# Planning the main slots and turning their first tokens inside the early slots, with early weights loaded at every second step

## The chip, the core and the metric

The kernel runs on one core of a Trainium2 chip. TensorE (PE) multiplies matrices; a weight load (PEld) goes ahead of each matmul. VectorE (DVE), ScalarE (ACT) and GpSimd (POOL) work on tiles, SyncE (SP) issues plain transfers, and POOL issues the indirect ones. Each engine works through its own queue in order. The metric is device time in microseconds (us) for one execution, lower is better.

## The reference

Linear attention over 8 batches, 8 heads, 576 tokens and 64 dimensions, followed by a mixture of 8 experts in which each token goes to one expert.

```python
def phi(x):                       # 64 -> 256 features
    proj = x @ w_phi
    proj = proj - max(abs(proj))
    return concat([exp(proj), exp(-proj)])
kv = phi(k).T @ v;  z = sum(phi(k))
attn = phi(q) @ kv / (phi(q) @ z + 1e-6)

x = attn as (8, 576, 512)
logits = x @ w_gate;  local = sigmoid(x @ w_local)
# token s of a batch: the argmax expert if s == 0 or local < 0.5,
# else the expert of the token before
p = softmax(logits)
out[b, s] = p[e] * (relu(x[b, s] @ w1[e]) @ w2[e])     # 512 -> 1024 -> 512
```

All numbers are float32. The kernel works the expert products as sums of three products of rounded parts (hi x hi, hi x lo, lo x hi).

## The kernel before

**Attention, 72 steps.** The tokens are handled in chunks of 128; 9 chunks make a pair of batches, and 4 pairs of batches by 4 pairs of heads give 144 chunks, two per `step`. A step projects (`proj`), turns, exponentiates (`qtr`, `qexp`), sums keys into values (`kv`), and takes matmuls of the numerator from a list (`num`); the result `xo` goes to HBM (`xs`), and POOL adds its gate columns to the logits `lg` (L421 to L424). In this stage PE's order is the program's.

**Gates.** When a pair of batches is done, `gate` runs as a generator in the background, one piece at a step (`chores`): the expert of each token, its rank among the tokens of that expert, its probability. POOL then scatters token numbers and probabilities into a list in HBM that is sorted by expert (`lst`, nine indirect transfers, L657). The fourth gate runs after the last step: `ends` keeps it as `last_gate`, and `advance` (called `go` in `run`) and `rest` push it on from inside the expert work.

**Early slots.** After the second gate half of the tokens have their experts. `plan_early` fills two slots (e0, e1) of three units of 128 tokens of one expert, to be worked while the rest is not yet known. It reads the list by an indirect gather into `lr` (`fetch`, L722), and turns the list with two PE transposes (L735) `WAIT` steps later. `early_chores` advances the early weights (`early_weights`) at each step: SP loads a piece of 512 KB into `wraw`, and one step later ScalarE copies the high part (`whi`, L935) and POOL subtracts for the low part (`wlo`, L937, four operations). The six gathers of tokens (`xg`, L964) follow, one per step. POOL's transfers in the background begin behind a small copy of the current step's maximum (`paced`, L518), so that they keep in step.

**Expert slots.** `slots` works through a list of slots: `layer1` (512 to 1024, relu into `hh` and its rest `hl`), `layer2` (1024 to 512, one PSUM tile `l2` for each unit, then `y` on VectorE and an indirect write to `out`, L1103). In pauses between matmuls these call functions from a list: the next slot's tokens are turned there (`tokens`, L990, into `xhi`, `xlo`), and what `run` passes in `soon` (pauses of the first layer) and `later` (behind the tokens, in the second layer). `used` and `spare` load and split the next slot's weights, one piece for each piece that is done with; 11 pairs of buffers in the early slots, 13 in the main ones. Into what memory a piece comes first also depends: with `ml1` open, every other `wraw` is there, in memory that the list tile had.

**Main slots.** `plan_main` starts from the final counts and works out, in about a hundred small VectorE operations (L745 to L866), which expert each of the main slots has and where its tokens stand, gathers the list again and turns it. Before, its first part was called at the last pause of e0's second layer and its second part at the fifth pause of e1's first layer. Then `moe` began: it gathered the first main slot's tokens, loaded its weights, turned its tokens, and went on with slots of 4, 3, 2 and 1 units.

Outside the 72 steps a planner orders each engine's queue ahead of time from the program's order and its own estimate of when inputs are ready, so a call's place in the program is the earliest, not always the final place of its instructions.

Of the kernel before, what the change touches and what calls it, by code (L numbers as in the profile page):

```python
# [7 lines left out]
F32 = mybir.dt.float32  # L8
# [19 lines left out]

GATE_T = -1.5 * 2.0 ** -23

WAIT, HOLD = 2, 2
PLACE = 16
LAG = 1
WE, WR, WL = 8, 3, 2
# [21 lines left out]
class Kernel:  # L56
# [9 lines left out]
    def run(self):  # L66
        nc, tc, A = self.nc, self.tc, self.A
        act, dve = self.act, self.dve
        with ExitStack() as root:
# [66 lines left out]
            front.close()  # L136
            self.open_main(root)
            plan = self.plan_main()

            def more():  # L140
                with tc.high_priority():
                    next(plan, None)
            go = self.advance

            def rest():
                for _ in self.last_gate:
                    pass
            no = lambda: None
            self.slots(self.eslots, soon=[[no, no, no, go, no, no, go, no, no, go, rest], [no, no, no, no, more]],
                       later=[[no, no, more]])  # L150
            back.close()
            self.open_rest(root)
            self.moe()
# [228 lines left out]
    def num(self, u, b, cs, kvs, bank=None):  # L382
# [23 lines left out]
        def end():  # L406
            last()
            dve, pool, t = self.dve, self.pool, e["t"]
            for c in cs:
                del self.ch[u * NC + c]  # L410
            rc = self.back2.tile([128, 3, 2], F32, name="rc", bufs=3)[:, 0:n]
            dve.tensor_scalar_add(rc, t[:, :, DEN], 1e-6)
            dve.reciprocal(rc, rc)
            xo = self.back2.tile([128, 3, 2 * KV], F32, name="xo", bufs=4)[:, 0:n]
            dve.tensor_mul(xo.rearrange("p c (h k) -> p c h k", h=2), t.rearrange("p c (h k) -> p c h k", h=2),
                           rc.unsqueeze(3).broadcast_to([128, n, 2, KV]))
            if hp == 0 and c0 == 0:
                self.lg[bp] = self.back2.tile([128, NC, 9], F32, name="lg")
            lg, ga, gb = self.lg[bp][:, c0:c0 + n], xo[:, :, 0:9], xo[:, :, 2 * KV - 9:2 * KV]
            if hp == 0:  # L420
                pool.tensor_add(lg, ga, gb)  # L421
            else:
                pool.tensor_add(lg, lg, ga)
                pool.tensor_add(lg, lg, gb)  # L424
# [18 lines left out]

    def early_chores(self, s, f):

        w = self.early_weights()
        for x in f:
            next(w, None)
            yield x
        for x in s:  # L450
            for u in range(x["n"]):
                with self.paced():
                    self.gather_x(x, u)
                next(w, None)
                yield STEP
        for _ in w:
            yield STEP
# [54 lines left out]
    def paced(self):  # L512


        if self.tail:
            return nullcontext()
        t = self.small.tile([128, 1], F32, name="tick", bufs=2)
        return self.tc.issue_after(self.pool.tensor_copy(t, self.m[:, 0:1]).ins)  # L518

# [16 lines left out]
    def gate(self, bp):  # L536
# [9 lines left out]
            return ap.unsqueeze(1).broadcast_to([128, NC, E])  # L546

        lt = self.lg.pop(bp)
        L = lt[:, :, 0:E]
        mx = sm([128, NC], "mx")  # L550
        dve.tensor_reduce(mx, L, AX.X, ALU.max)
# [148 lines left out]
    def fetch(self, es, k, n, name, wait, halves=()):  # L700
# [11 lines left out]
            yield STEP  # L712
        full = n
        if halves:
            n, halves = n + DUALS, halves()
        lr = self.small.tile([NU + DUALS, 128 * PLACE], F32, name="lr")[0:n]
        parts = [(lr[0:full], 128, ri[0:full, :])]
        w = 64 * PLACE
        parts += [(lr[full:n, w * z:w * z + w], 64, r[0:DUALS, :]) for z, r in enumerate(halves)]
        for o, b, r in parts:  # L720
            with self.paced():
                ins = pool.indirect_dma_start(o, None, self.lst.rearrange("(u n) t -> u (n t)", n=b),  # L722
                                              bass.IndirectOffsetOnAxis(r, 0))
            for x in self.scattered:
                self.tc.add_manual_dep(ins.ins, x.name, mybir.DependencyInfo(
                    mybir.DependencyClass.Sync, mybir.DependencyReason.DATA), reason="the list is read")
        self.scattered = []
        for _ in range(wait):
            yield STEP
# [61 lines left out]
    def plan_main(self):  # L791
# [75 lines left out]
            return rh  # L867

        f = self.fetch(es, k, NU, "m", 1, duals)
        next(f)  # L870
        yield
        try:
# [4 lines left out]
        self.by_size = {}  # L877
        for n, cap in SIZES:
            self.by_size[n], at = [], FIRST[n]
            for i in range(cap):  # L880
                self.by_size[n].append(dict(ei=[ei[at:at + 1]], tok=tok, prob=prob, u=at, n=n, name=f"m{at}", rows=NT + 1))
                at += n
        self.ds = [dict(ei=[x[i:i + 1] for x in eh], tok=tok, prob=prob, u=NU + i, n=1, name=f"d{i}", rows=NT + 1)
                   for i in range(DUALS)]


    def open_main(self, root):
# [193 lines left out]
    def layer2(self, s, between, held=None):  # L1081
        tc, dve, pool = self.tc, self.dve, self.pool
        hh, hl = s["h"]
        for k in range(s["n"]):
            self.l2n = getattr(self, "l2n", 0) + 1
            p = self.psr if hasattr(self, "psr") and self.l2n % 3 else self.psm4
            t = p.tile([128, DM], F32, name="l2")
            o = slice(k * 128, k * 128 + 128)
            for f in range(8):
                c = slice((f % 2) * DM, (f % 2) * DM + DM)  # L1090
# [20 lines left out]

    def slots(self, order, held=None, soon=(), later=()):
        first = order[0]
        for f in self.tokens(first):
            f()
        self.held = len(first.get("w", ()))
        self.coming = list(order)
        for i, s in enumerate(order):
# [149 lines left out]
```

## Time and profile before

| | us |
|---|---|
| runs, each alone | 771.33, 777.69, 777.87 |
| median of these | 777.69 |
| profiled execution, whole | 769.31 |
| its span, first to last instruction | 767.5 |
| TensorE busy in the span | 738.5 |
| VectorE, ScalarE, POOL busy | 449.8, 342.6, 181.8 |
| mean granted TensorE clock | 0.991 |

The profile is one execution. A row of a timeline gives the start, the duration, the engine, the line of the kernel, the operation with output and inputs, and in brackets the time that the engine stood idle ahead of it with what ended the idle time. In the windows each engine's busy time in a stretch is followed by the granted clock (1.00 is full speed) and by the share of time for which the 16 DMA engines were busy. Matmuls overlap, so the duration of one is more than its share of time.

### The profile page before, as it was taken

What the parts mean: (1) busy time and instruction counts of PE and PEld (TensorE: products, weight loads), DVE (VectorE), ACT (ScalarE), POOL (GpSimd) and SP (SyncE); (2) the same over time, 40 slices, a digit from 0 to 9 for tenths busy, and PEclk for the clock granted to TensorE, in tenths of its full rate; (3) what the DMA queues carried; (4) which work ended last, traced back from release to release, by engine and by line L of the source; (5) the groups of instructions that cost most, each with busy time, mean ns of one, the idle gap of its engine ahead of it and who ended that gap; (6) DMA issues with size and microseconds to landing.
All of it is one profiled execution on the core that took longest, in us unless ns stands there. A gap on an engine that the chain in (4) does not pass through costs nothing. (4 is left out here: it accounts for less than half of the span.)

```text
span 767.5 us, 21973 instructions
## 1 busy us (share of the span) xinstructions
PE 738.5 (96%) x9319; PEld 636.8 (83%) x9319; DVE 449.8 (59%) x828; ACT 342.6 (45%) x648; POOL 181.8 (24%) x307
## 2 busy tenths in 40 slices
PE   7999999999897999998999999999999999999996
PEld 6999989989897988887768985788888778878895
DVE  5888888789886887564652247435323554544411
ACT  4776667656785574313541136314212453433300
POOL 0210103301595441525302130021202102101011
PEclk9999999999998999999999999999999999999999
DMA  7755545544777614115923977432397464432000
GB/s 201 239 169 141 152 122 147 154 126 138 238 227 233 188 38 127 65 43 196 364 90 110 358 293 267 150 124 82 124 352 282 142 243 165 138 123 97 1 38 29
DMA packets 66100, 125.04 MB, mean 163 GB/s; under 512 B 7220, under 2 KB 45300, under 8 KB 65950
## 3 DMA queue, kind: packets, MB, share of 16 engines
q1 hardware_dynamic: 57808, 101.03, 40.5%
q0 software_dynamic: 8016, 22.51, 8.3%
q8 instruction: 74, 1.21, 0.6%
q14 instruction: 26, 0.21, 0.1%
q10 hardware_dynamic: 176, 0.07, 0.0%
HBM read 102.05 MB, written 22.06 MB: 162 GB/s over the span
## 5 line engine op out<-in xcount | busy, mean ns | idle before, releaser
L935 ACT CAST whi<-wraw 128x1024 fp32r<-128x1024 f32 x88 | 92.1, 1048 | 127.2 <-PE l L1005 51.9
L937 DVE TENSOR_TENSOR wlo<-wraw,whi 128x1024 fp32r<-128x1024 f32 x80 | 97.7, 1224 | 86.7 <-ACT whi L935 86.7
L1004 PE MATMUL l<-xhi,whi 128*128 128x384 f32 (+2 forms) x352 | 126.0, 358 | 2.2 <-DVE hl L1044 1.8
L1006 PE MATMUL l<-xhi,wlo 128*128 128x384 f32 (+2 forms) x352 | 123.9, 352 | 0.0
L1005 PE MATMUL l<-xlo,whi 128*128 128x384 f32 (+2 forms) x352 | 123.6, 351 | 0.0
L1004 PE MATMUL l<-whi,hh 128*128 128x512 f32 x288 | 117.4, 407 | 2.4 <-DVE y L1100 1.6
L1006 PE MATMUL l<-whi,hl 128*128 128x512 f32 x288 | 114.4, 397 | 0.0
L1005 PE MATMUL l<-wlo,hh 128*128 128x512 f32 x288 | 114.2, 396 | 0.0
L276 ACT ACTIVATE kp<-sb 128x512 f32<-128x512 f32 x144 | 83.7, 629 | 57.9 <-DVE sb L272 55.1
L270 DVE TENSOR_REDUCE m<-pj 128x8 f32<-128x1024 f32 x72 | 87.8, 1219 | 36.0 <-PE pj L267 34.4
L1043 ACT ACTIVATE hh<-l 128x384 fp32r<-128x384 f32 (+1 forms) x84 | 44.9, 534 | 132.4 <-PE l L1006 132.4
L300 ACT ACTIVATE qp<-pj 128x512 f32<-128x512 f32 x144 | 80.3, 596 | 33.6 <-PE pj L285 10.4
L267 PE MATMUL pj<-first,kq 64*128 64x128 f32 x1152 | 86.9, 292 | 6.9 <-DMA kq<-in_kqT 4.1
L272 DVE TENSOR_TENSOR sb<-pj,m 128x1024 f32<-128x1024 f32 x72 | 88.1, 1224 | 3.4
L395 PE MATMUL nm<-kvs,qp 128*64 128x74 f32 x2304 | 87.5, 229 | 1.4 <-ACT kvs L375 1.4
L1044 DVE SCALAR_TENSOR_TENSOR hl<-l,hh 128x384 fp32r<-128x384 f32 (+1 forms) x84 | 51.4, 612 | 59.4 <-ACT hh L1043 59.4
L267 PEld LDWEIGHTS pj<-first,kq 64*128 64x128 f32 x1152 | 73.0, 194 | 13.9 <-ACT ks L364 4.3
L395 PEld LDWEIGHTS nm<-kvs,qp 128*64 128x64 f32 x2304 | 80.1, 138 | 2.4 <-ACT kvs L375 2.1
L317 PE MATMUL kvp<-v,kp 128*64 128x65 f32 x2048 | 78.8, 228 | 1.4 <-issue 0.9
L1004 PEld LDWEIGHTS l<-xhi,whi 128*128 128x128 f32 x352 | 66.1, 188 | 16.7 <-issue 5.2
L1103 POOL DMA_INDIRECT out<-y,p_tokm x30 | 34.4, 1147 | 179.7 <-DVE y L1100 164.7
L317 PEld LDWEIGHTS kvp<-v,kp 128*64 128x64 f32 x2048 | 68.4, 140 | 5.3 <-ACT kp L276 1.4
(222 smaller groups left out, 922.5 us busy)
## 6 DMA issues: line engine op xcount, KB each, us to landing
wraw<-in_w1h SPq DMA_DIRECT2D x44, 512.0 KB, 6.6
wraw<-in_w2h SPq DMA_DIRECT2D x44, 512.0 KB, 3.7
kq<-in_kqT SPq DMA_DIRECT2D x47, 384.0 KB, 4.0
v<-in_va SPq DMA_DIRECT2D x48, 195.0 KB, 3.7
xs<-xo SPq DMA_DIRECT2D x48, 128.0 KB, 3.4
whi<-in_w1h SPq DMA_DIRECT2D x8, 512.0 KB, 7.0
wlo<-in_w1h SPq DMA_DIRECT2D x8, 512.0 KB
whi<-in_w2h SPq DMA_DIRECT2D x8, 512.0 KB, 4.0
```

The source lines that it names most:

```text
L267: self.last_pe = self.pe.matmul(t[:, h, i % 2, j, :], kq[r, j, s], self.w2[r], start=True, stop=True)
L270: dve.tensor_reduce(m, f, AX.X, ALU.max, apply_absolute_value=True)
L272: self.last_dve = dve.tensor_sub(sb.rearrange("p h c j f -> p (h c j) f"), f, m.unsqueeze(2).broadcast_to([128, 8, 128]))
L276: self.last_act = act.activation(kp[:, :, :, sg, :].rearrange("p c h f -> p h c f"), sb[:, :, :, 0], AF.Exp, scale=1.0 - 2 * sg)
L300: self.act.activation(qp[:, sg].rearrange("p h (c r k) -> p (h c) r k", c=2, r=2), src, AF.Exp, scale=1.0 - 2 * sg)
L317: self.pe.matmul(t[r, sg, h], kp[:, h, sg, r], v[:, h], start=first and sg + h == 0, stop=last and sg + h == 2)
L395: self.pe.matmul(e["t"][r, c - c0, k], self.ch[i]["qp"][:, sg, h, q0 + r.start:q0 + r.stop], kvs[:, sg, k], start=sg == 0, stop=sg == 1)
L935: self.act.copy(hi, raw)
L937: (low or self.dve).tensor_sub(lo[:, c], raw[:, c], hi.bitcast(F32)[:, c])
L1004: mm(o, ah, bh, start=first, stop=False)
L1005: mm(o, ah, bl, start=False, stop=False)
L1006: self.last_pe = mm(o, al, bh, start=False, stop=last)
```

## The change

The plan's first two parts are called at the first pause of e0's second layer (`listed`), which also puts the first main slot on the list of slots whose weights come next; its third part (`read`) at the third pause of e1's first layer; the first main slot's tokens are gathered at the fifth (`ahead`) and turned in e1's second layer from the third pause on. Functions in `later` now come ahead of the next slot's tokens. `slots` turns its first slot's tokens only if that has not been done. The slots' descriptions are made before the list is fetched, and the gathers for the half units are issued behind the full one. The second layer's tile of the early slots comes from the pool `psb` (two banks) and no longer from `psm4` (one bank). The early weights advance at every second step, `WAIT` is 3, a gate's first part waits one more step during attention, and after the last step `paced` puts transfers behind the last logit addition.

```diff
-WAIT, HOLD = 2, 2
+WAIT, HOLD = 3, 2
...
-            def more():
-                with tc.high_priority():
-                    next(plan, None)
...
+            def listed():
+                next(plan)
+                next(plan)
+                self.coming.append(self.by_size[4][0])
+
+            def read():
+                with tc.high_priority():
+                    next(plan, None)
             no = lambda: None
-            self.slots(self.eslots, soon=[[no, no, no, go, no, no, go, no, no, go, rest], [no, no, no, no, more]],
-                       later=[[no, no, more]])
+            m = []
+
+            def ahead():
+                m.append(self.tokens(self.by_size[4][0], True))
+            self.slots(self.eslots, soon=[[no, no, no, go, no, no, go, no, no, go, rest], [no, no, read, no, ahead]],
+                       later=[[listed], [no, no] + [lambda k=k: m[0][k]() for k in range(4)]])
...
-                pool.tensor_add(lg, lg, gb)
+                self.last_pool = pool.tensor_add(lg, lg, gb)
...
-        w = self.early_weights()
+        w, k = self.early_weights(), 0
         for x in f:
-            next(w, None)
+            if k % 2 == 0:
+                next(w, None)
+            k += 1
             yield x
...
-                next(w, None)
+                if k % 2 == 0:
+                    next(w, None)
+                k += 1
                 yield STEP
...
         if self.tail:
-            return nullcontext()
+            return self.tc.issue_after(self.last_pool.ins)
...
         lt = self.lg.pop(bp)
+        if not self.tail:
+            yield STEP
...
+        gather(lr[0:full], 128, ri[0:full, :])
+        if halves:
+            for z, r in enumerate(halves()):
+                gather(lr[full:n, w * z:w * z + w], 64, r[0:DUALS, :])
...
         f = self.fetch(es, k, NU, "m", 1, duals)
+        self.by_size = {}
...
+        yield
         next(f)
         yield
...
-            p = self.psr if hasattr(self, "psr") and self.l2n % 3 else self.psm4
-            t = p.tile([128, DM], F32, name="l2")
+            if hasattr(self, "psr"):
+                t = (self.psr if self.l2n % 3 else self.psm4).tile([128, DM], F32, name="l2")
+            else:
+                t = self.psb.tile([128, DM], F32, name="l2", tag="nm")
...
-        for f in self.tokens(first):
-            f()
+        if "x" not in first:
+            for f in self.tokens(first):
+                f()
...
             if i < len(later):
-                rest = rest + list(later[i])
+                rest = list(later[i]) + rest
```

More of the change, by code (lines that the diff above doesn't have):

```diff
@@ L714, in fetch, with gather @@
         if halves:
-            n, halves = n + DUALS, halves()
+            n = n + DUALS
         lr = self.small.tile([NU + DUALS, 128 * PLACE], F32, name="lr")[0:n]
-        parts = [(lr[0:full], 128, ri[0:full, :])]
         w = 64 * PLACE
-        parts += [(lr[full:n, w * z:w * z + w], 64, r[0:DUALS, :]) for z, r in enumerate(halves)]
-        for o, b, r in parts:
+        def gather(o, b, r):
             with self.paced():
@@ L869, in plan_main @@
         f = self.fetch(es, k, NU, "m", 1, duals)
+        self.by_size = {}
+        for n, cap in SIZES:
+            self.by_size[n], at = [], FIRST[n]
+            for i in range(cap):
+                self.by_size[n].append(dict(ei=[ei[at:at + 1]], u=at, n=n, name=f"m{at}", rows=NT + 1))
+                at += n
+        yield
         next(f)
@@ L876, in plan_main @@
         self.tok, self.prob, self.eim, self.eih = tok, prob, ei, eh
[L877 to L884, printed above, removed]
+        self.ds = [dict(ei=[x[i:i + 1] for x in eh], u=NU + i, n=1, name=f"d{i}", rows=NT + 1) for i in range(DUALS)]
+        for x in [x for n, _ in SIZES for x in self.by_size[n]] + self.ds:
+            x.update(tok=tok, prob=prob)
     def open_main(self, root):
```

## The prediction

> **What bounds the kernel now.** I read the page's totals first, then PE's busy time in long and in short windows, then what ended PE's waits, and last the queues that feed those waits.
>
> ```profile
> span 767.5 us, 21973 instructions
> PE 738.5 (96%) x9319; PEld 636.8 (83%) x9319; DVE 449.8 (59%) x828; ACT 342.6 (45%) x648; POOL 181.8 (24%) x307
> ```
>
> TensorE is the bound: it is busy for 738.5 of 767.5 us, so all that an edit of order can win lies in 29 us of gaps, and in time that PE spent at a lower clock. The windows (PE, PEld, DVE, ACT, POOL busy, then granted clock and DMA share) say where these are.
>
> ```profile
> 205.00:235.00 30.00, 28.24 (x721) 26.65 (x721) 21.15 (x34) 24.64 (x51) 28.46 (x53) 1.00 0.77 235
> 235.00:240.00 5.00, 1.41 (x24) 1.06 (x22) 4.93 (x15) 1.30 (x3) 2.83 (x5) 0.82 0.98 325
> 240.00:245.00 5.00, 5.00 (x74) 4.85 (x74) 2.38 (x7) 2.39 (x5) 1.43 (x3) 0.50 0.57 175
> 300.00:400.00 100.00, 93.03 (x456) 77.94 (x456) 59.26 (x173) 37.11 (x52) 31.27 (x29) 0.98 0.42 151
> 360.00:365.00 5.00, 2.47 (x15) 1.81 (x14) 3.74 (x5) 3.23 (x5) 4.39 (x3) 0.95 1.01 372
> 365.00:370.00 5.00, 5.00 (x17) 4.00 (x16) 2.67 (x3) 1.77 (x2) 1.25 (x2) 0.71 1.03 409
> 400.00:760.00 360.00, 359.87 (x1814) 293.38 (x1813) 145.63 (x177) 110.23 (x162) 56.84 (x52) 1.00 0.46 165
> ```
>
> From 400 to 760 us PE is full at full clock: the main slots end a fixed time after they start, so whatever is won ahead of 400 us moves the end one for one. Two places lose. **Place A**, 205 to 245, is where the early weights are loaded: POOL is busy 28.46 of 30 us, then PE has a hole, and after the hole 5 us at half clock. **Place B**, 300 to 400, is the two early slots and the passage to the main slots: 100 - 93.03 = 6.97 us without PE work, and clocks of 0.95 and 0.71 in two windows.
>
> Place A in the timelines of PE, POOL and DVE, with the tile queries of lr and g_rs (columns of a timeline: start, duration, what, and in brackets the idle time ahead of it and what ended it):
>
> ```profile
> 236.18 0.46 PE L285 MATMUL pj<-first,sb 64*128 64x64 f32 x8 [0.91 <-DVE sb L272]
> 236.48 0.29 PE L285 MATMUL pj<-first,kvs 64*128 64x64 f32 x4
> 239.45 0.38 PE L735 MATMUL pj<-first,lr 6*128 6x6 f32 x2 [2.68 <-DMA lr<-lst,p_rie]
> ```
> ```profile
> 230.15 2.80 POOL L937 TENSOR_TENSOR wlo<-wraw,whi 128x256 fp32r<-128x256 f32 x4
> 232.88 0.19 POOL L518 COPY tick<-m 128x1 f32<-128x1 f32 x1
> 233.24 0.92 POOL L722 DMA_INDIRECT lr<-lst,p_rie  x1 [0.17 <-issue]
> ...
> 234.69 2.92 POOL L937 TENSOR_TENSOR wlo<-wraw,whi 128x256 fp32r<-128x256 f32 x4
> ```
> ```profile
> 234.76 0.23 DVE L551 TENSOR_REDUCE g_mx<-lg 128x9 f32<-128x72 f32 x1 [2.46 <-POOL lg L424]
> ...
> DMA to landing us min/median/max: 2.6/2.7/6.2
> ...
> L561 DVE SCALAR_TENSOR_TENSOR g_rs<-lg,consts x4: 161/161/697, 89.8 to 299.7; 128x9 f32<-128x9 f32 x4
> ```
>
> PE stands 2.68 us for the early list: the gather left POOL only at 233.24, right behind a split of 2.8 us on an engine without a gap, and took 6.2 us to land, the longest of its kind. DVE stood 2.46 us at the head of a gate for logits that POOL had queued behind the same splits, which cost PE 0.91 us.
>
> **The change, place A.** Three edits. (1) The early weights go on at every second step: the same 8 loads, 8 ScalarE copies and 8 POOL splits, over twice the steps. Per pair of steps POOL loses one 2.8 us split, so the gather leaves when it is due and not about one split (2.8 us) late. (2) WAIT 3 puts the two transposes (L735) one step further on; the four gates stand 18 steps apart, and g_rs runs in the first at 89.8 and in the last at 299.7: 209.9 / 54 = 3.9 us per step. Needed: 2.68 us. Given: 3.9 + 2.8 = 6.7. The slack is 4.0 us, and the landing is unlikely to be slower than 6.2 us, since that row already lies in a stretch with DMA share 0.98. The 2.68 us go, with them the half clock: 5 us at 0.50 is 2.5 us of work lost. (3) A gate begins one step later, so its first reduce finds the logits: 0.91 us. Together 2.68 + 2.5 + 0.91 = **6.1 us**. Later now are the six token gathers, by two steps, and the last splits, by about eight: they end near 205 + 17 x 3.9 = 271, and the early slots need them only about when the last gate begins, at 299.7. Some 25 us cover them; without that cover each step of delay would cost 3.9 us.
>
> The rest of 205 to 235 had 30 - 28.24 = 1.76 us of idle PE. If ScalarE's copy costs PE in each step that has one, nothing of it is won; if the backlog did it, all: 0 to 1.76, I take 0.9. Against it: a gate now runs beside splits that are not yet done. The third gate, begun at 234.76, lay beside the split at 234.69: its g_rs took 697 ns, against 161 ns in the others, 0.54 more. With a split (2.8 us) in every 7.8 us, a gate's dozen such small operations meet one about four times: 0 to 2.1 us of DVE, part of it covered; I take 0.6. Net **+0.3 us**, ends -2.1 and 1.8.
>
> At the clock stands a rule that speaks against half of this. By the Trainium skill, "TensorE: Matmul & The Clock Gate", Part 1, PE falls to half clock only after an idle window of some 3.4 us. By that rule a hole of 2.68 us, and the shorter ones of place B, would cost no clock, and the sum would lack 2.5 + 1.7 us. The rows above disagree: clock 0.50 stands right behind 0.91 + 2.68 us of idleness, 0.71 behind the smaller holes below. I go by the rows, and keep the rule as a rival.
>
> On g_rs the rule of "GPSIMD Engine Reference", Specifications, agrees: GpSimd shares its SBUF interfaces with VectorE and contends with instructions that have two SBUF inputs. It gives no price, so the sum stays with the 0.54 us.
>
> **The change, place B.** What ended PE's waits from 305 to 405 (us in total, times, longest):
>
> ```profile
> PE tr L990 <- DMA xg<-xs,p_tokm: 2.5, 2, 1.7
> PE l L1004 <- DVE hl L1044: 1.8, 2, 1.7
> PE l L1004 <- DVE y L1100: 1.6, 2, 0.8
> PE l L1004 <- DVE p_r L822: 0.8, 1, 0.8
> ```
>
> With the 0.2 us of L735 (its row is below) these sum to 6.9, the whole gap. The rows behind them, of the tile lst, then of PE, SP, POOL, DVE (with the landing of xg) and ACT:
>
> ```profile
> L657 POOL DMA_INDIRECT lst<-pr,ri x36: 954/994/1512, 120.4 to 324.0; - x36
> ...
> 332.88 0.21 PE L745 MATMUL pt<-cnt,consts 128*44 128x8 bf16 x2
> ...
> 352.62 0.39 PE L735 MATMUL pt<-first,lr 48*128 48x48 f32 x2 [0.21 <-DMA lr<-lst,p_rim]
> ```
> ```profile
> 353.14 2.97 SPq L925 DMA_DIRECT2D wraw<-in_w1h  x4
> ```
> ```profile
> 347.50 0.96 POOL L722 DMA_INDIRECT lr<-lst,p_rim  x1 [4.49 <-DVE p_rim L707]
> 353.54 0.98 POOL L964 DMA_INDIRECT xg<-xs,p_tokm  x1 [5.07 <-DVE p_probm L738]
> ```
> ```profile
> 312.18 0.16 DVE L646 TENSOR_TENSOR cnt<-g_cs,cnt 128x8 bf16<-128x8 f32 x1
> ...
> DMA to landing us min/median/max: 3.2/5.0/8.8
> ```
> ```profile
> 350.02 0.49 ACT L1043 ACTIVATE hh<-l 128x384 fp32r<-128x384 f32 x1 [1.59 <-PE l L1006]
> ...
> 381.27 1.05 ACT L935 CAST whi<-wraw 128x1024 fp32r<-128x1024 f32 x1 [3.85 <-DMA wraw<-in_w1h]
> ```
>
> The plan starts at 332.88 although the counts stood at 312.18. Moved from the last pause of the first early slot's second layer to its first one, it passes 54 second-layer matmuls (360 / 1814 = 0.2 us each by the last window), 12 transposes and the waits between: 11 + 3 = 14 us sooner, near 319; expert numbers and list gather by 333.5, transposes near 338.5, token gathers from 339.5. They carry the same instructions; the two half-unit gathers now follow the full one (1.3 us each). Four token gathers 1.3 us apart (an estimate from 0.98 us each), the last landing at most 8.8 us after issue, are there by 353. The second early slot's second layer, which now turns them, begins behind its last first-layer tiles, of which hh at 350.02 is one, and turns them from its third pause on: the 2.5 us go. The main slot's 8 loads no longer wait for the list's memory to be free (the SP row at 353.14 follows the list's transposes at 352.62); they start by 333.5 and have some 35 us, so the DMA engines need not be full (share 1.01 and 1.03) just where the tokens are fetched. The second layer's sum goes to a pool of two banks in place of one: its waits for the row y and for the plan's operations ahead of y (1.6 + 0.8) go, since one bank is read out while the other is filled for a whole unit.
>
> The 1.8 us behind hl come from ScalarE standing 3.85 us for a weight of the second main slot, with hh queued behind it. That slot's loads are still early and in a bunch, though alone: I keep half, 0.9, and the list's 0.2. New waits are likely somewhere, since ScalarE, VectorE and SP now do the main weights in the second early slot: I take 1.2, between 0.8 and 1.7 of the waits above. The clock's part: 0.05 x 5 + 0.29 x 5 = 1.7 us, all gone. **6.9 + 1.7 - 1.1 - 1.2 = 6.3 us**, ends 8.6 (nothing kept, nothing new) and 1.1 (a hole with half clock as in place A, 5.2, on top). The order edges in the tail (gathers behind the last addition on POOL) cost nothing: the last gate begins with that addition done, at 299.7, and its scatters need what DVE works out after 312.
>
> **Sum.** 6.1 + 0.3 + 6.3 = 12.7 us. The profiled execution took 769.31 us, so 756.6. The three runs shown are 771.33, 777.69 and 777.87, between 2.0 and 8.6 above it; nothing in the profile says what the others lost, but stalls followed by a slow clock are where one run can lose more than another. I add 4.4, about half: **761 us**, 2.1% under the median.
>
> **Rivals.**
> (a) *The stall moves.* PE's queue is in order; the list's or the tokens' transposes may now stand in the second early slot ahead of their data, as L735 did in place A. For: scatters, three list gathers and weights meet there. Against: L735 stood only 0.21 us in place B before. Price: a hole of 2.7 and half clock of 2.5, 5.2 us: 766 us.
> (b) *Slower: ScalarE blocks in the second early slot.* Its hh comes every 2.1 us (1.59 idle + 0.49) and has slack of about one such tile. Now 8 weight copies stand between. If each waits for its load as the copy at 381.27 did (3.85), PE loses 3.85 - 2.1 = 1.75 at each, and with PE at half clock as much again: 8 x 3.5 = 28 us against 12.7 won, 773.7 - 12.7 + 28 = 789 at worst. It decides from 1.6 us lost per load, 12.7 in all. For: the copy's row. Against: the DMA share over 300 to 400 is 0.42 with the burst in it, and the main slots do the same with PE full.
> (c) *The plan isn't really earlier.* The list gather waits for the last gate's nine scatters, which POOL issues until 324.0, and for a DVE chain (332.88 to the gather at 347.50, 14.6 us) that has no raised priority now. Then place B stays, A goes: 769.3 - 6.4 + 4.4 = 767 us.
> (d) *Half clock isn't tied to these holes.* Then its 2.5 + 1.7 us fall elsewhere as the holes go, and 8.5 us are won: 765 us. For: 0.71 stands behind holes of 1.7 and 0.8 us alone. Against: no window in 400 to 760 lost clock, where PE had no hole. That is the rule of "TensorE: Matmul & The Clock Gate" in the Trainium skill, weighed above.
>
> **Chances.** Forecast 0.52 (its own range 753 to 769), (a) 0.18, (b) 0.09, (c) 0.13, (d) 0.08. A measurement of this kernel can tell about 1% from no change, given runs 0.8% apart. Below 769.9 lie nearly all of the forecast and most of (a), (c) and (d): 0.69; within 1%: 0.21; slower: 0.10. The range reaches from the sum with no run offset and 4 us more won, 752, over (a), (c), (d) with the full offset, 775.
>
> **What would show it.** The list's transposes in place A without a wait and no window at half clock there; L745 near 313 to 315 (the whole is 6 us sooner); SP's main loads in one thin row from 325 to 330, not a burst; no wait on xg; l2 in its new banks with no wait on y; PE full from about 290 to the end. Wrong would be: a new hole between 325 and 375 with a clock under 0.9, ScalarE waiting for wraw with hh behind it, or a PE order in which the plan's matmuls come no sooner than before.

## The result, and the profile after

| | before | changed | ratio, 95% interval |
|---|---|---|---|
| first chip, median | 775.08 us (10 runs, 771.33 to 777.87) | 768.66 us (10 runs, 766.18 to 770.29) | 0.9917 [0.9897, 0.9936] |
| profiled execution | 769.31 (span 767.5) | 768.59 (span 766.8) | |
| second chip (runs after_again and before) | 769.2 | 763.11 | 0.9911 [0.9886, 0.9937] |
| third chip (after_3) | 768.28 | 763.34 | 0.9929 [0.9902, 0.9956] |

The change is faster, by 0.7 to 0.9% or 5 to 7 us; the prediction's sum had 12.7 us, and its forecast of 761 us lies 7.7 under the 768.66 measured. The experiments ran on further chips, of two kinds: the kernel before takes 768 to 769 us on some and 774 to 775 us on the others, the first among these. The profiled execution of 769.31 us lies below all ten runs of the kernel before on the first chip; on which chip it ran is not on record. All ratios are against the kernel before on the same chip. Ratios are those of the means without three runs in a much slower state (811.72, 1428.69 and 1429.26 us), which move no median given here by more than 0.3 us.

The page of the changed kernel, first chip:

```profile
span 766.8 us, 21974 instructions
PE 739.7 (96%) x9319; PEld 637.3 (83%) x9319; DVE 451.0 (59%) x828; ACT 344.5 (45%) x648; POOL 181.9 (24%) x306
```

The same windows as before (PE, PEld, DVE, ACT, POOL busy, granted clock, DMA share, GB/s):

```profile
205.00:235.00 30.00, 28.98 (x718) 26.91 (x714) 22.82 (x38) 20.92 (x45) 17.76 (x37) 1.00 0.71 208
235.00:240.00 5.00, 4.07 (x90) 3.40 (x88) 3.92 (x12) 3.48 (x7) 3.81 (x6) 1.00 0.51 150
240.00:245.00 5.00, 4.22 (x116) 3.79 (x117) 3.60 (x7) 3.87 (x10) 0.22 (x1) 1.00 0.76 234
300.00:400.00 100.00, 95.77 (x467) 81.56 (x465) 60.19 (x178) 35.45 (x50) 31.90 (x33) 0.97 0.45 151
340.00:345.00 5.00, 1.80 (x9) 1.42 (x9) 1.89 (x2) 1.16 (x2) 1.00 (x1) 0.89 0.93 322
345.00:350.00 5.00, 5.00 (x16) 4.59 (x16) 4.39 (x7) 3.33 (x5) 2.17 (x3) 0.50 0.67 213
360.00:365.00 5.00, 4.99 (x26) 4.34 (x25) 3.36 (x5) 2.87 (x5) 0.00 (x0) 1.00 0.73 252
400.00:760.00 360.00, 359.82 (x1815) 293.15 (x1814) 146.60 (x177) 112.61 (x164) 59.35 (x53) 1.00 0.47 166
```

Both old holes are filled: 235 to 240 holds 4.07 us of PE work (1.41 before), the clock is 1.00 in 240 to 245 (0.50), and 360 to 365 is full (2.47). But 340 to 350 is a new hole with half clock behind it, and 240 to 245 at full clock has gaps where the half clock had none.

Place B in what ended PE's waits from 305 to 405, with the rows behind them from the timelines of PE, SP and POOL:

```profile
PE pt L753 <- DMA lr<-lst,p_rim: 3.2, 1, 3.2
PE l L1024 <- DVE g_es L617: 0.6, 1, 0.6
PE l L1024 <- DVE hl L1064: 0.5, 1, 0.5
```
```profile
319.82 0.18 PE L763 MATMUL pt<-cnt,consts 128*44 128x8 bf16 x1
...
344.23 0.42 PE L753 MATMUL pt<-first,lr 48*128 48x48 f32 x2 [3.20 <-DMA lr<-lst,p_rim]
```
```profile
335.56 6.75 SPq L945 DMA_DIRECT2D wraw<-in_w1h  x4
```
```profile
336.87 1.50 POOL L736 DMA_INDIRECT lr<-lst,p_rim  x1 [0.31 <-issue]
```

The plan starts at 319.82 (332.88 before), and no wait on xg or on the row y is left. The list's gather, the last of three, is issued at 336.87 behind four main weight loads that SP began at 335.56; it lands near 344, and PE stands 3.20 us ahead of the list's transposes (L753, which was L735).

### The profile page after: what moved, and what is told of

Its sections match the earlier page's. It is cut to its first block, busy times and chain, and to the rows that moved or that the text cites. A ratio compares the mean times of both kernels' runs of the same rounds, so it can differ in the third digit from the quotient of the medians.

```text
span 766.8 us, 21974 instructions
## 1 busy us (share of the span) xinstructions
PE 739.7 (96%) x9319; PEld 637.3 (83%) x9319; DVE 451.0 (59%) x828; ACT 344.5 (45%) x648; POOL 181.9 (24%) x306
## 5 line engine op out<-in xcount | busy, mean ns | idle before, releaser
L276 PE MATMUL pj<-first,kq 64*128 64x128 f32 x1152 | 85.8, 290 | 8.0 <-DMA kq<-in_kqT 4.2
L276 PEld LDWEIGHTS pj<-first,kq 64*128 64x128 f32 x1152 | 72.2, 192 | 15.1 <-issue 5.2
```

The lines of the kernel that those rows point to most:

```text
L276: self.last_pe = self.pe.matmul(t[:, h, i % 2, j, :], kq[r, j, s], self.w2[r], start=True, stop=True)
```

## The experiments

"Step n" begins at row n of the projections (pj<-first,kq) in PE's timeline, counted from 0; the first row holds two projections. "71" is the first l<-xlo matmul, with which the first layer of the first early slot begins. "The third gate's transpose" is the matmul that turns g_code. The main half is the part of the change in the early slots, the attention half the part in the 72 steps and at their end. "Like chips" are chips of the same kind.

**1. Each half alone, the kernel before again, and a hold.** The attention half alone, against the kernel before (WAIT 3, early weights at every second step, the gate's later start, the order behind the last sum; the second place of the weights' count and the last sum's lines are left out here):

```diff
-WAIT, HOLD = 2, 2
+WAIT, HOLD = 3, 2
...
-            next(w, None)
+            if k % 2 == 0:
+                next(w, None)
+            k += 1
...
+        if not self.tail:
+            yield STEP
...
```

> Only the part of the change in the attention stage: WAIT 3, early weights at every second step, a gate one step later, transfers of the tail behind the last logit addition; plan and first main tokens as before. Theory 1 (the hole at the early list goes, but the list's transposes now share a step with a gate's first transpose, and gates run beside splits): the wait on the list is gone at step 60 of 72 and 4 to 5 us are won there, of which 4 to 5 are lost again by step 70; 0 to 2 us faster than before in all. Rival (place A is a clean gain and place B takes it away): 5 to 6 us faster, about 769 to 770.

Measured: 768.78 beside 769.19, ratio 1.0001 [0.9986, 1.0017]. The attention half is not told apart from no change; the interval leaves room for some 1.3 us either way. The main half alone (the plan, the tokens and the banks as changed, the lines above as before):

> Only the part in the early slots: plan, list and first main tokens earlier, second layer in two banks; attention stage as before. Theory 1 (the main slot's weights now start with the list gather and delay it; the hole moves from the tokens to the list's transposes): a wait of 2 to 4 us on the main list with a window at half clock behind it, the waits on xg, y and hl gone; 2 to 6 us faster than before. Rival (nothing is won in place B): within 1 us of before.

Measured: 761.97, ratio 0.9891 [0.9873, 0.9910]. The main half alone gives as much as the whole change, with the wait on the early list (2.46 us) still there. The kernel before, for its profile:

> The kernel before, unchanged, for a second profile of it. The first one took 769.3 us while its other runs lie between 771.3 and 777.9 with a median of 775.1. Theory 1 (the profiled execution was a lucky one): a second profile shows about 775, with some 5 us more of idle time or half clock in 200 to 400 us, most likely a longer wait for the early list or for the first main tokens. Theory 2 (a profiled execution is always faster than the others for this kernel): again about 769, with the same holes.

Measured: 769.14, span 767.4; the wait on the early list was 2.02 us, that on xg 2.8 us, and the clock 0.62 in 240 to 245. The other runs on this chip have a median of 769.19, so a profiled execution of 769 is no exception on it. Then the changed kernel with the main slot's first load held until the three list gathers have landed (the lines cut here add a dependence of the load on each of them):

```diff
+            if s["name"] == "m0":
+                for x in self.behind:
...
```

> The changed kernel, with the first main slot's first weight load held until the main list's three gathers have landed; nothing else. Theory 1: the list lands in 3 to 4 us in place of 6 to 7, the wait of 3.2 us in front of its transposes shrinks under 1 us and the half clock behind it (345 to 351 us) goes: 4 to 6 us faster than the changed kernel, about 763 to 765. Rival (the list is late because of the scatters or its own issue, not of the weights): the wait stays, and holding the weights costs up to 2 us.

Measured: 762.37, ratio 0.9900 [0.9884, 0.9917]. The hole goes, as the window and the PE row of this run (hold) show; the third row is the main half alone (b_only), whose gather also leaves just behind the burst:

```profile
340.00:345.00 5.00, 5.00 (x30) 4.70 (x29) 1.44 (x4) 1.23 (x3) 2.48 (x4) 1.00 0.67 236
341.19 0.42 PE L757 MATMUL pt<-first,lr 48*128 48x48 f32 x2
```
```profile
340.81 0.39 PE L747 MATMUL pt<-first,lr 48*128 48x48 f32 x2 [1.58 <-DMA lr<-lst,p_rim]
```

So the burst of weights is what makes the gather late: held, the slowest of the three list gathers lands 4.8 us after its issue, against 7.0 in the main half alone. But the time falls by only 0.7 us against the changed kernel on a like chip (763.11), inside both intervals and not the 4 to 6 expected. The loads now start later, at 341.13, and from 305 to 405 PE waits 2.0 us for hl, against 0.7 in the changed kernel on that like chip.

**2. Which part of the attention half gives the time back.** The main half with the hold (attention as before), then the attention half alone with two wait steps, the same with three and the weights at full pace, and the changed kernel again.

> The attention part as in the kernel before, the main part as in the change, and the first main slot's first weight load also behind the landing of the list gathers. If the burst of main weights beside the list gather is what the new hole costs (about 4 us from step 71 to the end, 463.3 against 467.3 in the changed kernel with and without it), and the attention part as it was has no loss of its own: step 71 as before (about 297.5 on the trace), 463 us behind it, span about 761, time 758 to 761 and ratio 0.985 to 0.990. If the hold only moves the hole (the loads, started later, make the first main slot late): as the main part alone, about 762, ratio 0.991.

Measured: 761.93, ratio 0.9894 [0.9874, 0.9914], no different from the main half without the hold (0.9891). On chips of this kind the hole is real, and its price in the median is not seen; the intervals leave room for some 2 us.

The attention half of the first experiment, with two wait steps:

```diff
-WAIT, HOLD = 3, 2
+WAIT, HOLD = 2, 2
```

> The attention part of the change alone, but with two steps between the list gather and its transposes, so that these come a step ahead of the third gate's first transpose again. If the coincidence of both in step 61 is what gives the won time back (6.24 us for that step instead of 3.93): step 61 falls to about 4 us, the list transposes wait in step 60 (up to 2.7 us, if the gather lands no earlier), step 71 comes 1 to 2 us earlier than with the attention part alone, time about 767 beside 769, ratio 0.997. If the time is given back by the gate's vector operations beside the splits: no difference from the attention part alone, 769, ratio 1.000.

Measured: 766.96, ratio 0.9970 [0.9952, 0.9988]; step 61 takes 4.12 us (248.94 less 244.82) where the attention half with three wait steps has 6.25. This is what was expected if the two meet at a cost. Step 60 takes 6.15 us in place of 5.52, so part of the 2.1 us goes there.

The attention half of the first experiment, with the early weights at every step (at both places of the count):

```diff
-            if k % 2 == 0:
-                next(w, None)
-            k += 1
+            next(w, None)
```

> The attention part of the change alone, but with the early weights loaded at every step as before: left of it are the third wait step, the gate's later start and the end behind the last sum. The splits of these weights on POOL and ACT then end some steps earlier and lie less beside the third gate. If the third gate's vector operations beside the splits cost the time (5.3 us for step 64 to 65 against 3.8): that step falls by 1 us or more, time about 767, ratio 0.997. If the coincidence of transposes and gate is the cause: step 61 is still about 6 us and the time about 769, ratio 1.000. If slower early weights are what moved the list gather forward (its landing 2.7 us earlier relative to its transposes): a wait on the list of 0.5 to 2 us comes back, time 770 to 772.

Measured: 769.88, ratio 0.9999 [0.9981, 1.0016]; step 61 is 6.24 us, step 64 4.52 (5.31 with the slower weights), and the list is there in time. But step 59 takes 6.94 us (4.81 with the slower weights), with PE waiting 2.27 us for sb, because VectorE again stands 3.35 us for POOL's logits. Full pace wins 0.8 us in step 64, loses more in step 59, and wins nothing in all.

> The changed kernel once more, for a second profile beside one of the kernel before on one chip. If the 2.7 us that it loses between steps 49 and 71 against the kernel before are its own: that stretch is about 106 us again (103 before), ratio 0.992. If they came from the one execution: about 103 to 104, with the same ratio, and the profile then says little about single microseconds of this stretch.

Measured: 763.11, ratio 0.9911. Steps 49 to 71 take 104.2 us, not 106.3: 2.1 us of what the first profile lost there belong to that execution or chip.

**3. Single edits on the main half, and the half clock by itself.** The run warm: nine matmuls whose result is not used (128x12, into the bank that the transposes overwrite) in the wait on the early list of the kernel before:

```diff
...
+                for _ in range(9):
+                    self.last_pe = self.pe.matmul(t.rearrange("p a b -> p (a b)"), self.ident, self.ident[:, 0:2 * n], start=True, stop=True)
```

> The kernel before, with nine small matmuls whose result is not used (128x12 numbers each) put ahead of the early list's transposes, so that TensorE has work in the wait on the list and may keep its clock. The wait itself stays. If the half clock behind the wait costs what the prediction put down for it (2.5 us): granted clock 1.00 in 240 to 260, steps 60 and 61 fall from 5.4 and 3.9 to about 4 and 3.7, time about 767, ratio 0.997. If those steps are as long at full clock (the changed kernel's step 60 is 5.52 us at full clock, before 5.44 at half), the vector engine or the chain between the engines sets them: step 60 stays at 5.3 to 5.5, time 769, ratio 0.999 to 1.001. If the nine take longer than the wait: up to 1 us more.

Measured: 775.16 beside 774.38, ratio 1.0010 [0.9990, 1.0029]. Inconclusive: PE had no pause over 1 us, and the clock fell all the same (0.85 over 240 to 260, step 60 5.61 us):

```profile
240.00:260.00 20.00, 19.66 (x433) 18.38 (x434) 15.28 (x36) 9.98 (x24) 5.40 (x11) 0.85 0.60 174
```

These matmuls did not keep the clock, so the half clock's price was not isolated this way.

The changed kernel with two wait steps:

```diff
-WAIT, HOLD = 3, 2
+WAIT, HOLD = 2, 2
```

> The changed kernel with two steps between the early list's gather and its transposes instead of three, all else as changed. If the coincidence of transposes and third gate in step 61 is a loss of its own that adds up with the main part: step 61 of 4.1 instead of 6.2 us, time 1.5 to 2.5 us under the changed kernel, 761, ratio 0.988 to 0.989. If the main part's gain and this one overlap: 763, ratio 0.991.

Measured: 767.14 beside 774.38, ratio 0.9904 [0.9886, 0.9923], 0.1% under the changed kernel on other chips, and inside its interval. Step 61 falls to 4.13 us, but step 60 takes 6.88; the two outcomes that were expected are not told apart.

The main half with the slower early weights alone (b_pace); against the changed kernel:

```diff
-WAIT, HOLD = 3, 2
+WAIT, HOLD = 2, 2
...
-        if not self.tail:
-            yield STEP
...
-            return self.tc.issue_after(self.last_pool.ins)
+            return nullcontext()
```

> The main part of the change, and of the attention part only the early weights at every second step: two wait steps as before, the gate's start as before, no end behind the last sum. If the slower weights alone move the list's landing forward and everything else in that part is cost: no wait on the early list or one under 1 us, step 61 of 4 us, time 2 us under the main part alone, 759 to 760, ratio 0.987. If the slower weights cost what they win, because their splits then lie beside the third gate (step 64 of 5.2 instead of 3.8 us): as the main part alone, ratio 0.989 to 0.990.

Measured: 770.67, ratio 0.9955 [0.9939, 0.9971], a miss on both sides. The slower weights alone do take the wait on the early list away (0.19 us is left; steps 59 to 64 take 26.5 us, 30.1 and 30.6 in two runs of the main half alone), without a loss in step 61. But steps 65 and 66 then take 14.6 us in place of 6.7. PE's timeline, in rows of this run (the projections of steps 65, 66 and 67 are its L276 rows):

```profile
259.70 1.16 PE L276 MATMUL pj<-first,kq 64*128 64x128 f32 x16
...
264.46 0.36 PE L404 MATMUL nm<-kvs,qp 128*64 128x74 f32 x4 [0.32 <-issue]
265.19 0.39 PE L404 MATMUL nm<-kvs,qp 128*64 128x74 f32 x5 [0.36 <-issue]
...
269.47 2.08 PE L276 MATMUL pj<-first,kq 64*128 64x128 f32 x16
274.31 1.16 PE L276 MATMUL pj<-first,kq 64*128 64x128 f32 x16
```

PE works in bits of 0.4 us with waits between that end on nothing the profile shows ("issue"), and then slowly: the 16 matmuls that take 1.16 us elsewhere take 2.08.

The changed kernel without the gate's later start:

```diff
-        if not self.tail:
-            yield STEP
```

> The whole change without the gate's start one step later. The third gate then runs a step ahead of the list's transposes with their three wait steps, so that its first transpose is in step 60 and theirs in step 61. If only their meeting in one step costs: step 61 of 4 to 4.5 instead of 6.2 us, ratio 0.988 to 0.989. If the gate's later start is itself a gain (step 49 about 1 us earlier with it, but two gates follow before that): that 1 us is lost again and the ratio stays at 0.990 to 0.991.

Measured: 768.91, ratio 0.9936 [0.9916, 0.9956]. Step 60 takes 8.1 us: the third gate's transpose waits 1.28 us for the list's copy there. Without the later start both gate and list come a step earlier, so the meeting moved a step and did not end. From 250 to 300 us this run has 2.4 us of unexplained waits besides, so the ratio decides neither case.

**4. Before, main half, all, and two wait steps on one chip (before_3, b_only_2, after_3, wait2_2); then two single edits on another.**

> The kernel before, for a profile on the chip of the three others. If the sessions differ by TensorE's waits for nothing the profile shows: at a median near 775, 2 to 6 us of such waits in 250 to 300 us; at a median near 769, under 1 us.

Measured: 768.71, span 766.8, 0.8 us of unexplained PE waits in all, none of them in 250 to 300.

> The main part alone once more. If the attention part is worth nothing: ratio 0.989 as before, within 0.002 of the whole change's. If its worth hangs on the chip: at a median of before near 775, the whole change 2 us or more ahead of or behind this one.

Measured: 763.12, ratio 0.9921 [0.9890, 0.9951], span 761.6.

> The whole change beside its main part alone on one chip. If what the attention part wins comes back in the steps 61 to 65: ratio 0.990 to 0.992, the same as or 1 to 2 us behind the main part alone, and step 59 to 71 takes 63 to 64 us in both. If the attention part wins: 1 us or more ahead of it.

Measured: 763.34, ratio 0.9929 [0.9902, 0.9956], span 761.4. With the attention half or without it, the time is the same, by medians of 763.34 and 763.12 us.

> The whole change with two wait steps, beside the other two. If the coincidence of the list's transposes with the third gate's is a loss of its own: 1 to 2 us under the whole change, ratio 0.988 to 0.990. If not: the same as the whole change within 0.5 us.

Measured: 761.85, ratio 0.9916 [0.9886, 0.9946], 1.5 us under the changed kernel, as expected if the meeting is a loss of its own, though the intervals overlap. It is the best version here by its median on this chip; it is not told apart from the main half alone.

> The main part with the slower early weights alone, once more. If the unexplained waits around 265 us are this kernel's own: again 3 us or more of them in 250 to 300 us, step 65 to 67 takes about 14 us instead of 6.7, ratio 0.994 to 0.997, behind the main part alone (0.989 and 0.992). If they belong to the session: under 1 us of them, step 65 about 4 us earlier than with the main part alone, ratio 0.984 to 0.987.

Measured: 771.79 beside 773.99, ratio 0.9975 [0.9960, 0.9991]: the same waits in the same place (steps 65 and 66 in 14.6 us). Both runs were on chips of the 774 kind, and warm, the kernel before with nine matmuls more, had waits of this sort in its step 65 there (8.95 us); whether they are this kernel's or those chips' stays open.

The changed kernel with two wait steps and the early weights at every step, so that of the attention half the gate's later start and the order behind the last sum are left:

```diff
-WAIT, HOLD = 3, 2
+WAIT, HOLD = 2, 2
...
-            if k % 2 == 0:
-                next(w, None)
-            k += 1
+            next(w, None)
```

> The main part, and of the attention part only the gate's start one step later and the order behind the last sum; early weights at every step and two wait steps as before. If the later gate costs by itself, because its operations then lie beside the list's transposes and the splits: 1 us or more behind the main part alone, ratio 0.991 to 0.994. If it only takes VectorE's wait for the logits away: up to 1 us ahead of it, ratio 0.988 to 0.991. The wait on the early list of 2 to 2.7 us is still there in both.

Measured: 768.06 beside 773.99, ratio 0.9927 [0.9904, 0.9951]. The time stays within what the main half alone gave on other chips, so nothing is shown by it. The trace shows two things that neither case expected. The wait on the early list is gone, since the list's transposes stand a step later. In its place PE waits 2.24 us for sb, for VectorE stands 3.31 us for POOL's logits: with the weights at every step the gate's later start does not make its first reduction find them.

## Why the prediction was right in part

The step that failed is place A. The prediction booked 6.1 + 0.3 us there as a net gain, and the runs show none of it: the waits went, 4.2 us were won in steps 59 and 60, and the same 4.2 came back by step 71, where the moved operations met others.

**Place A (6.1 + 0.3 us): the wait went, the time did not.** PE's projections of steps 59, 60, 61, 62, 64 and 65 and the first of the early slot, in the kernel before (before_3) and then in the changed one (after_3), on one chip:

```profile
233.19 1.16 PE L267 MATMUL pj<-first,kq 64*128 64x128 f32 x16
242.25 1.92 PE L267 MATMUL pj<-first,kq 64*128 64x128 f32 x16
247.70 1.16 PE L267 MATMUL pj<-first,kq 64*128 64x128 f32 x16
251.63 1.16 PE L267 MATMUL pj<-first,kq 64*128 64x128 f32 x16
259.74 1.16 PE L267 MATMUL pj<-first,kq 64*128 64x128 f32 x16
263.55 1.16 PE L267 MATMUL pj<-first,kq 64*128 64x128 f32 x16
296.63 0.44 PE L1005 MATMUL l<-xlo,whi 128*128 128x384 f32 x1
```
```profile
233.33 1.16 PE L276 MATMUL pj<-first,kq 64*128 64x128 f32 x16
238.13 1.16 PE L276 MATMUL pj<-first,kq 64*128 64x128 f32 x16 [0.51 <-ACT ks L373]
243.65 1.16 PE L276 MATMUL pj<-first,kq 64*128 64x128 f32 x16
249.90 1.16 PE L276 MATMUL pj<-first,kq 64*128 64x128 f32 x16 [1.03 <-ACT ks L373]
257.79 1.16 PE L276 MATMUL pj<-first,kq 64*128 64x128 f32 x16
263.10 1.16 PE L276 MATMUL pj<-first,kq 64*128 64x128 f32 x16 [0.86 <-ACT qp L309]
296.78 0.44 PE L1025 MATMUL l<-xlo,whi 128*128 128x384 f32 x1
```

| step | before_3 | after_3 | difference |
|---|---|---|---|
| 59 | 9.06 | 4.80 | -4.26 |
| 60 | 5.45 | 5.52 | +0.07 |
| 61 | 3.93 | 6.25 | +2.32 |
| 62 and 63 | 8.11 | 7.89 | -0.22 |
| 64 | 3.81 | 5.31 | +1.50 |
| 65 to 71 | 33.08 | 33.68 | +0.60 |

What step 59 held in before_3:

```profile
235.43 0.47 PE L285 MATMUL pj<-first,sb 64*128 64x64 f32 x8 [1.07 <-DVE sb L272]
238.28 0.38 PE L735 MATMUL pj<-first,lr 6*128 6x6 f32 x2 [2.27 <-DMA lr<-lst,p_rie]
```

Step 59 sheds 4.26 us: these two waits (3.34; 2.68 and 0.91 were counted), and 0.9 that is left over and put down to the clock. So "5 us at 0.50 is 2.5 us" was mis-sized: step 60 is no shorter at full clock than with half clock at its start, with PE waiting 0.77 us for DVE's sb. What PE does faster there, it waits.

The term "ends -2.1 and 1.8, net +0.3" was wrong in its sign, and its list of new costs lacked the largest. Two things come back. In step 61 the list's transposes (L753) now meet the third gate's (L587). Rows of the changed kernel's profile (first chip), then of wait2_2, the same with two wait steps:

```profile
245.57 0.38 PE L753 MATMUL pj<-first,lr 6*128 6x6 f32 x2
246.81 0.28 PE L587 MATMUL pj<-first,g_code 128*9 128x128 f32 x1 [0.86 <-DVE p_probe L756]
...
250.35 1.16 PE L276 MATMUL pj<-first,kq 64*128 64x128 f32 x16 [1.03 <-ACT ks L373]
```
```profile
239.11 0.38 PE L753 MATMUL pj<-first,lr 6*128 6x6 f32 x2
...
244.39 0.28 PE L587 MATMUL pj<-first,g_code 128*9 128x128 f32 x1
```

The gate's transpose waits 0.86 us until DVE has copied the list out (p_probe), and everything queued behind it, with ACT's ks, is late by 1.03 more. The prediction counted the slack of the wait (4.0 us) and never asked what else lands in the step it moves to. It also had the move too short: the early plan follows the second gate, so that gate's later start moves the list by a step of its own. The transposes stand in step 59 before and in b_pace, in step 60 with either edit alone (b_gate, b_nostep), in step 61 with both; the third gate's stands in step 60 without the later start and in 61 with it. With two wait steps step 61 takes 4.1 us: in wait2_2 it begins at 242.93 and ends at 247.05. The medians are then 1.8 us less on the attention half and 1.5 on the whole change on like chips, and 0.1% on a chip of the other kind.

In step 64 the gate's operations lie beside a split, as the prediction said they might. Two rows of DVE in the kernel before's first profile, and then DVE and POOL in after_3, and last, from the same run, a copy of an early weight and a wait in step 67:

```profile
256.47 0.22 DVE L604 TENSOR_TENSOR g_oh<-g_es,consts 128x72 f32<-128x72 f32 x1
256.73 0.35 DVE L607 CAST g_ohb<-g_oh 128x72 bf16<-128x72 f32 x1
```
```profile
257.52 0.57 DVE L619 TENSOR_TENSOR g_oh<-g_es,consts 128x72 f32<-128x72 f32 x1
...
258.13 0.62 DVE L622 CAST g_ohb<-g_oh 128x72 bf16<-128x72 f32 x1
```
```profile
255.90 2.79 POOL L957 TENSOR_TENSOR wlo<-wraw,whi 128x256 fp32r<-128x256 f32 x4 [0.83 <-ACT whi L955]
```
```profile
271.83 1.03 ACT L955 CAST whi<-wraw 128x1024 fp32r<-128x1024 f32 x1
273.48 1.38 PE L404 MATMUL nm<-kvs,qp 128*64 128x74 f32 x36 [0.59 <-ACT kvs L384]
```

These are 0.62 us more for two operations, ahead of DVE's share of the step; ACT's qp, behind them, ends PE's wait of 0.86 us at 263.10. In a_full and b_gate, where the early weights are done by then, the two take 0.22 and at most 0.28 us and step 64 about 4.5: so of its 1.50 us more some 0.8 come with the slower weights and 0.7 with the gate's later start. The 0.60 of 65 to 71 lie in step 67, where PE waits 0.59 us for ACT's kvs, which is queued behind a weight copy that the slower pace has put there; in a_full and b_gate that step takes 4.04 in place of 4.98. The prediction took 0.6 for the gate's operations beside splits; of the other late splits and copies it asked only whether they are done by 299.7. Steps 64 to 71 show 2.1. At the first matmul of the early slot the changed kernel is 0.15 us behind, from 0.14 behind at step 59, so of 6.4 us nothing is left. In the pair of first profiles (769.31 and 768.59 us) the changed kernel even loses 1.9 us here (65.63 after 63.70).

**Place B (6.3 us): right in size.** From that matmul to the end of the span it is 470.2 us before (766.8 - 296.63) and 464.6 changed (761.4 - 296.78): 5.6 won, within the ends 1.1 and 8.6; the main half alone won 5.2 to 7.2 us by its medians. PE's waits from 305 to 405 sum to 7.0 us there before and 2.1 changed; the prediction had left 1.1 and added 1.2. In the pair of first profiles the stretch gains only 2.4 (469.7 and 467.3). The steps came as told: the plan 13 us sooner, no wait on xg or y, PE full from 360 on. Two details were wrong. The new waits did not come from ScalarE or VectorE but from the list, rival (a), with 3.20 us where the prediction spoke against it by the 0.21 us before. And SP's loads are no thin row: "they start by 333.5" was right within 2 us (335.56), and just that put them in the gather's way; before, they began only behind the list's transposes (353.14). Its price of 5.2 us is too high for the chips of the 769 kind: there the hole is 1.6 to 2.5 us in this kernel and its main half, and to remove it changes the median by 0 to 0.7 us. On the first chip it is 3.20 us with a window at half clock behind it, and the stretch to the end is 2.4 to 2.7 us longer than in the changed kernel on the other two; the hold never ran on a chip of that kind, so what the hole costs there stays open.

**The run offset (4.4 us): near, by luck.** The sum ended at 756.6. Without place A that is 763.0, and the changed kernel takes 763.1 and 763.3 on chips where the kernel before takes 768 to 769, which is where its profiled execution (769.31) lies. On the first chip both medians are higher (775.08, 768.66). The prediction took half of the spread of three runs, with no cause for it; what it met is a difference of some 5 to 6 us between two kinds of chips. Of the 7.7 us by which the forecast of 761 misses, 6.4 are place A; the other 1.3 are less than place B alone differs by between the two pairs of profiles (5.6 and 2.4). And the 2.1% were counted from the three runs' median of 777.69, which ten runs put at 775.08.

**Rivals.** (b) and (c) did not occur: no copy of ScalarE held PE in place B, and the plan is earlier. (a) came as a hole, at the price told above. (d) is near in place A: the half clock went and most of its time was not won. That the clock is not tied to PE's pauses alone, as warm showed with work in the hole, counts against how the prediction read the row 240 to 245. In the changed kernel 3.20 us of waiting were followed by clock 0.50, and in warm the clock is 0.85 over 20 us with no pause over 1 us. The rule on the clock's idle window in the Trainium skill ("TensorE: Matmul & The Clock Gate", Part 1, some 3.4 us) does not fit these rows either.

## What to carry to other kernels

A stall that is removed from an in-order queue pays only what the next limit leaves: here step 60 kept its 5.5 us when the clock came back, with TensorE waiting for VectorE in it. When work is moved by a step, list what already stands in the step it moves to, and on which shared buffer. A transfer that was held back by accident may have been protecting a small, late gather; look what it will now start beside, and measure what that costs before it is mended: here the hole was real and its removal hardly showed in the time.

## What the runs showed of the hardware that was not expected

PE at times waits in bits of 0.2 to 1.1 us for nothing the profile shows, in several runs on chips of the 774 kind (1.8 to 4.2 us in 250 to 300 in six of the seven profiles taken there of kernels other than the one before) and less on the others (1.04 us in hold, under 0.6 in the rest). They fall in different steps in different kernels. What causes them stays open.

Matmuls of 12 columns, back to back for 2.6 us, did not prevent the half clock in warm. On one chip, a wait of 2.51 us in the main half alone (b_only_2) was followed by windows at clock 1.00, and one of 1.63 us in the changed kernel (after_3) by 0.66 over 5 us. So the length of a pause alone did not foretell the clock here.
